# Hand-set ScalarE order in the first product of a token mixer, and sums moved to three places

## The chip, the cores and the metric

The kernel runs on one core of a Trainium2 chip. The time is device microseconds (us) of one execution; lower is better. The engines are TensorE (PE: matmuls, and PEld: its weight loads), VectorE (DVE), ScalarE (ACT), GpSimd (POOL) and SyncE (SP), which issues nearly all DMAs here. Matmuls write to PSUM, eight banks of 128 partitions x 512 fp32 values; VectorE and ScalarE read and write it too.

## The reference

The inputs are bf16: x of 2048 tokens x 1024 channels, and weights. A linear-attention block comes first, then a mixer over the tokens:

```python
x = A_x
h = x + _A_ref(_layernorm(x), A_wqkv, A_wo)        # 32 heads of 32, linear attention
h2 = h + _B_ref(_layernorm(h), B_w1, B_b1, B_w2, B_b2)

def _B_ref(x, w1, b1, w2, b2):
    h = _layernorm(x)
    u = einsum("bsd,sf->bdf", h, w1) + b1          # S=2048, F=3584, D=1024
    u = gelu(u)                                    # tanh form
    y = einsum("bdf,fs->bds", u, w2) + b2
    return y.transpose(0, 2, 1)
```

The change lies in the first of the mixer's two products, `u = gelu(h w1 + b1)`, called mixer 1 below. The second, with w2, is mixer 2.

## The kernel before

The attention block takes the first 236 us of the profiled execution, mixer 1 runs from there to about 399 us, and mixer 2 to the end.

**Seven products.** Both mixer products are cut into 2 x 2 blocks and done with seven block products in place of eight (the Winograd form of Strassen's scheme). `Product7` holds one such scheme for a pair of 128-row tiles of the output: p1 to p7, each with its left operand (weights, or sums of weights made by VectorE with `asums`) and its moving operand (the halves `hE`, `hO` of the normalized h, or their differences `hT2` to `hT4`). The accumulators are the PSUM tiles A, B and C of 512 columns. In mixer 1, p1 is in both A and B. B then takes p6 and becomes the start of C by a ScalarE copy (`copy_c`, L362). C takes p7. p5 is kept in `e`. VectorE adds `e` to C or B (`with_shared`, L425), and ScalarE's GELU (`evac`, L419) writes the finished quarter to `gE` or `gO`.

**Two at a time, and once more seven.** A `Quad` holds two such schemes, `sts[0]` and `sts[1]`. Four of its seven products, numbers 1, 5, 2 and 3, are themselves done with seven smaller products over both schemes (`Inner`, and `Inner2` for numbers 2 and 3). These are the inner products `in1`, `in5`, `in2`, `in3`. Each has steps i1 to i7 of 4 matmuls with 256 columns. The tile name in the profile is psI. The steps are chained by ScalarE: i1's result is copied to a second accumulator (L258), i6 accumulates onto it and is copied to a third (L262), and i7 accumulates onto that. i5's result is copied to SBUF (`es`, L271), or added by VectorE in `Inner2`. The ends are the `sink` functions: ScalarE copies or VectorE sums into A and B (L493, L494, L499), into `e` (L502), or into fp32 tiles `t1` (profile name t1a) and `t3` (profile name t). VectorE makes the left operands of each inner product with `sums` (profile name is, 0.4 us each). The moving operands of an inner product come from four sums of a quarter of h (`inner_moving`; for `in3` these four are `sums3`: profile names hi and hO, in the order t3, b12, t2, t4). They are made once, in the first quad of `run1`.

**The stretch.** Since steps i1 to i7 wait for each other through ScalarE, `interleave` fills the waits with the matmuls of p4, p6 and p7, which are not done in seven (512 columns each; p4 is that of the quad before). Its order is

```python
n.i1, "in", 0, n.i6, n.i2, 1, n.i5, n.i7, flush, 2, "mid", n.i3, "third", 3, n.i4, "out", flush
```

where 0 to 3 are the parts of the fill, the names are places at which the caller may put work, and `flush` does the evacuations that finished fill products have put in the list `late`. A quad u in `run1` has four such stretches: `in1` with p4 of the quad before, `in5` with three quarters of p6, `in2` with the rest of p6 and the first half of p7, `in3` with the rest of p7. Between `in2` and `in3` the code has `sts[1].with_shared(...)` and the next quad's `begin1()`, which makes two `is` sums. There are seven quads: the first in `run_first`, u = 1 to 6 in `run1`.

**Order.** The framework's scheduler orders each engine's instructions by its own estimate of readiness, except those that are passed through `pin` (`keep_in_program_order`), which are placed behind what the code has issued on that engine before. `Held` wraps an engine so that its operations are pinned while `Held.on` is set. In mixer 1 that is so for VectorE (`dve`) and TensorE (`pe`). ScalarE's are issued as `nc.scalar`, and the scheduler is free with them. Most rows of wrapped operations carry line L217 in the profile.

Of the kernel before, what the change touches and what calls it, by code (L numbers as in the profile page):

```python
# [30 lines left out]
def kernel(  # L31
# [12 lines left out]
    nc = tc.nc  # L44
# [5 lines left out]
    CW = min(BANK, D)  # L50
# [34 lines left out]
    pin = tc.keep_in_program_order  # L85
# [68 lines left out]
    def load_w2(p, pool):  # L154
        w2_tiles[p] = w_tile(pool, WLEN if pool is wpool else NF * 2 * P)[:, 0:NF * 2 * P].rearrange("p (k f) -> p k f", f=2 * P)
        nc.sync.dma_start(
            w2_tiles[p],
            B_w2[:, p * 2 * P:(p + 1) * 2 * P].rearrange("(k p) s -> p k s", p=P),
        )
# [47 lines left out]
        return {1: b11, 2: b21, 3: b22, 4: t4, 5: b12, 6: t2, 7: t3}, sums  # L207

    class Held:
        on = False  # L210

        def __init__(self, engine, always=False):
            self.engine, self.always = engine, always

        def __getattr__(self, name):
            op = getattr(self.engine, name)
            return (lambda *a, **kw: pin(op(*a, **kw))) if self.always or Held.on else op  # L217

    dve, pe = Held(nc.vector), Held(nc.tensor)
    hv, ht, hs, hd = (Held(e, True) for e in (nc.vector, nc.tensor, nc.scalar, nc.sync))  # L220

    class Inner:
# [27 lines left out]
        def i1(self):  # L250
            ae = psz.tile([P, BANK], F32, tag="z0", bufs=1, name="psI0")
            bc = psz.tile([P, BANK], F32, tag="z1", bufs=1, name="psI1")
            e, c = ae, bc
            if self.banks == 4:
                e, c = (psw.tile([P, BANK], F32, tag="w", name=f"psI{i}") for i in (2, 3))
            self.a, self.e, self.b, self.c = ae[:, 0:HW], e[:, HW:CW], bc[:, 0:HW], c[:, HW:CW]
            self.mm(1, self.a, True)
            nc.scalar.copy(self.b, self.a)  # L258

        def i6(self):  # L260
            self.mm(6, self.b, False)
            nc.scalar.copy(self.c, self.b)  # L262

        def i2(self):
            self.mm(2, self.a, False)
# [2 lines left out]
        def i5(self):  # L268
            self.mm(5, self.e, True)
            self.es = cpool.tile([P, HW], F32, tag="es", name="es")  # L270
            nc.scalar.copy(self.es[:], self.e)  # L271

        def i7(self):
            self.mm(7, self.c, False)
# [23 lines left out]
    class Product7:  # L298
# [45 lines left out]
        def p1(self):  # L344
            self.begin()
            self.mm(1, self.A, True)
            nc.scalar.copy(self.B[:], self.A[:])

        def shared_tile(self):
            self.e = cpool.tile([P, BANK], F32, tag=f"e{self.p % 2}", name="e1")  # L350
# [1 line left out]
        def p5(self, ks=None):  # L352
            if ks is None or ks[0] == 0:
                self.E = psz.tile([P, BANK], F32, tag=f"z{self.p % 2}", bufs=1, name="psE1")
            self.mm(5, self.E, True, ks)
            if self.whole(ks):
                self.shared_tile()
                nc.scalar.copy(self.e[:], self.E[:])

        def copy_c(self):  # L360
            self.C = psy.tile([P, BANK], F32, tag="y", name="psC1")
            nc.scalar.copy(self.C[:], self.B[:])  # L362

        def p6(self, ks=None, late=None):
            self.mm(6, self.B, False, ks)
# [20 lines left out]
        def p7(self, cut=None):  # L386
            self.mm(7, self.C, False)
            self.parts = [(0, CW, self.C)]
            if cut is not None:
                self.parts = [(0, cut, self.C), (cut, CW, psw.tile([P, BANK], F32, tag="w", name="psC2"))]  # L390
                nc.scalar.copy(self.parts[1][2][:, cut:CW], self.C[:, cut:CW])
            self.evac_shared(1, self.C)

        def p3(self):
# [17 lines left out]
    class Mixer1(Product7):  # L412
# [3 lines left out]

        def evac(self, fh, dh, ps, a=0, b=CW):
            ft = 2 * self.p + fh
            nc.scalar.activation(  # L419
                (gE if fh == 0 else gO)[:, self.p, dh * CW + a:dh * CW + b],  # L420
                ps[:, a:b], ACT.Gelu_apprx_tanh, bias=b1_sb[:, ft:ft + 1], scale=1.0,
            )
# [59 lines left out]
    class Quad:  # L482
# [7 lines left out]

        def sink1(self, m, h, ps):
            A, B, c = self.sts[m].A, self.sts[m].B, self.cols(h)
            nc.scalar.copy(A[:, c], ps)  # L493
            nc.scalar.copy(B[:, c], A[:, c])  # L494

        def sum1(self, m, h, ps, es):
            A, B, c = self.sts[m].A, self.sts[m].B, self.cols(h)
            dve.tensor_tensor(A[:, c], ps, es, ALU.add)
            nc.scalar.copy(B[:, c], A[:, c])  # L499

        def sink5(self, m, h, ps):
            nc.scalar.copy(self.sts[m].e[:, self.cols(h)], ps)  # L502

        def sum5(self, m, h, ps, es):
            dve.tensor_tensor(self.sts[m].e[:, self.cols(h)], ps, es, ALU.add)
# [1 line left out]
        def steps(self, *fs):  # L507
            return [(f, k) for f in fs for k in range(self.sts[0].nk)]

        def interleave(self, n, steps, at={}):  # L510
            t = len(steps)
            cuts = [0, (5 * t + 8) // 16, (9 * t + 8) // 16, (12 * t + 8) // 16, t]

            late = []

            def fill(q):
                for f, part in groupby(steps[cuts[q]:cuts[q + 1]], lambda s: s[0]):
                    f([k for _, k in part], late)

            def flush():  # L520
                while late:
                    late.pop(0)()

            for f in (
                n.i1, "in", 0, n.i6, n.i2, 1, n.i5, n.i7, flush, 2, "mid", n.i3, "third", 3, n.i4, "out", flush,
            ):
                if isinstance(f, int):
                    fill(f)
                else:
                    (at.get(f, nop) if isinstance(f, str) else f)()  # L530
# [100 lines left out]
                dve.tensor_tensor(base[:, m, c], ps, base[:, m, c], ALU.add)  # L631
            return sink

        def run1(self, pend, nxt, on_p4, before_third=nop):
            sts = self.sts
            s4, s6, s7 = self.steps(*[st.p4 for st in pend]), self.steps(*[st.p6 for st in sts]), self.steps(*[st.p7_fill for st in sts])
            c6, c7 = 3 * len(s6) // 4, len(s7) // 2

            def starting():
                self.in1.sums(slice(2, 4))  # L640
                self.asums(5)
                self.in5 = Inner(sts, 5, self.mov5, "i5", self.sink5, self.sum5)
                self.in5.sums(slice(0, 2))
                self.asums(6)
                self.t1 = self.base("t1a")
                for s, st in enumerate(sts):
                    st.begin(self.t1[:, s, :])

            self.interleave(self.in1, s4, {"in": starting, "mid": lambda: self.in5.sums(slice(2, 4))})
            self.asums(7)  # L650
            in2 = Inner2(sts, 2, self.mov2, "i1", self.add_to(self.t1), None)
            in2.sums()
            on_p4()
            nxt = nxt()
            for st in sts:
                st.shared_tile()
            self.interleave(self.in5, s6[:c6])
            sts[0].finish()
            self.asums(3)
            self.base3()  # L660
            in3 = Inner2(sts, 3, self.mov3, "i5", self.add_to(self.t3), None)
            in3.sums()
            before_third()
            sts[0].with_shared(sts[0].base3, sts[0].B)
            self.interleave(in2, s6[c6:] + s7[:c7], {
                "third": lambda: sts[0].evac(0, 0, sts[0].A), "out": lambda: sts[1].evac(0, 0, sts[1].A),
            })
            sts[1].with_shared(sts[1].base3, sts[1].B)
            if nxt is not None:
                nxt.begin1()  # L670
            self.interleave(in3, s7[c7:], {
                "third": lambda: sts[0].evac(0, 1, sts[0].base3), "out": lambda: sts[1].evac(0, 1, sts[1].base3),
            })
            return sts, nxt

    def moving(E, O, T2, T3, T4):
# [11 lines left out]
    with ExitStack() as actx:  # L688
# [21 lines left out]
        with ExitStack() as a1:  # L710
# [455 lines left out]
            for q in range(2, NVP):  # L1166
                for R in (KRun, VRun):
                    n = R(q)
# [28 lines left out]
            for b in range(NKB):  # L1197
                j0, n = b * KPB, min(KPB, ND - b * KPB)
# [28 lines left out]
        with ExitStack() as a3:  # L1227
# [143 lines left out]
            for n, (u, j) in enumerate(q_units[8:]):  # L1371
# [14 lines left out]
                if n in sums_at:  # L1386
                    cur = next(ahead)
# [58 lines left out]
    mov3, sums3 = inner_moving(hO[:, :, CW:D], NSP, inner1, "hi3")  # L1446
    NQ1 = NFP // 2

    def next_load1(u):
        def load():  # L1450
            if u < NQ1:
                load_w1(u, 0)
                load_w1(u, 1)
            else:
                load_w2(0, wpool)
        return load

    def quad1(u):
        return Quad([Mixer1(2 * u), Mixer1(2 * u + 1)], mov1, mov5, mov2, mov3)

    Held.on = True
    sums5()
    cur.mov5 = mov5
    pend, nxt = cur.run_first(quad1(1), sums1, sums2)
    for u in range(1, NQ1):
        cur = nxt
        pend, nxt = cur.run1(pend, lambda: quad1(u + 1) if u + 1 < NQ1 else None, next_load1(u + 1), sums3 if u == 1 else nop)
    Held.on = False
    for st in pend:
        st.p4()  # L1470
    mctx.close()
# [11 lines left out]
    cur = Mixer2(0)  # L1483
# [42 lines left out]
    pend = [cur, Mixer2(1)]  # L1526
    nxt = quad2(1)
# [26 lines left out]
    for u in range(1, NSP // 2):  # L1554
        cur = nxt
        last = 2 * u + 2 == NSP
        pend, nxt = cur.run2(
            pend, lambda: None if last else quad2(u + 1), after_p4(u), make_t4, CW - P if last else None,
        )
# [32 lines left out]
```

## Time and profile before

| | |
|---|---|
| median of 3 executions | 569.0 us (568.55 to 570.59) |
| the profiled execution's own time | 569.72 us |
| its span, first to last instruction | 567.9 us |
| PE / DVE / ACT busy over the span | 98% / 76% / 49% |
| granted TensorE clock | 1.00 |
| a middle quad of `run1`, from `in5`'s i6 to the next one's (312.52 to 335.38) | 22.86 us: PE 22.75, DVE 19.33, ACT 12.29 busy |
| the first quad of `run1` (264.20 to 289.66) | 25.46 us |

In a row of a timeline, the first number is the start in us from the span's start, the second the time taken; then engine, line, operation, output tile, inputs, shapes, and in brackets how long the engine stood idle before it and who released it. In a row of the waits: engine, line and tile that waited, whom for, us in total, times, longest. Matmuls are pipelined, and the last one's shown end is modelled; the distance from start to start is the surer number. In the stream a matmul of 512 columns takes 0.2165 us from start to start.

### The profile page before, as it was taken

How to read it: one execution, taken by the hardware profiler on the slowest of the kernel's cores; microseconds unless marked ns; L12 is line 12 of the kernel's file. 1: busy time of each engine (PE TensorE's matmuls, PEld its weight loads, DVE VectorE, ACT ScalarE, POOL GpSimd, SP SyncE). 2: the span in 40 equal slices, each digit the busy share in tenths (PEclk: the TensorE clock that was granted, in tenths of full speed). 3: DMA queues.
4: the chain of work that ended last, by engine and by line, in shares of the span. 5: the costliest groups of instructions: out<-in, count | busy, mean ns of one | idle time of the engine just before them, and what ended most of it. 6: DMA issues, size and time to landing. Idle time of an engine off the chain costs nothing.

```text
span 567.9 us, 8564 instructions
## 1 busy us (share of the span) xinstructions
PE 557.9 (98%) x3215; PEld 303.8 (53%) x3215; DVE 431.6 (76%) x822; ACT 280.9 (49%) x597; POOL 1.8 (0%) x8
## 2 busy tenths in 40 slices
PE   8999999999999999999899999999999999999997
PEld 3444444454444444456566766666445645645643
DVE  6898888544776788887989789788979749658725
ACT  4647777766766877635456465464220411311211
POOL 1000000000000000000000000000000000000000
PEclk9999999999999999999999999999999999999999
DMA  8833332115764852104040440422992922912111
GB/s 302 292 75 74 75 89 42 19 47 195 213 205 130 267 171 81 67 1 145 6 148 5 145 141 9 149 66 66 226 237 88 262 78 74 292 43 74 38 47 46
DMA packets 86089, 67.15 MB, mean 118 GB/s; under 512 B 15762, under 2 KB 80032, under 8 KB 86048
## 3 DMA queue, kind: packets, MB, share of 16 engines
q1 hardware_dynamic: 85312, 65.94, 40.1%
q10 hardware_dynamic: 672, 0.66, 0.3%
q8 instruction: 25, 0.41, 0.3%
q14 instruction: 16, 0.13, 0.1%
q0 software_dynamic: 64, 0.01, 0.0%
HBM read 54.54 MB, written 8.91 MB: 112 GB/s over the span
## 4 chain that ended last, share of the span: by engine, by line
PE 85%; DVE 9%; ACT 2%; DMA 2%; issue 1%; SPq 1%; DVEq 0%; ACTq 0%
PE acc_t L217 18%; PE psI L217 15%; PE psC L217 11%; PE psB L217 10%; PE psA L217 4%; PE psB L854 4%; PE psC L854 4%; PE psA L854 4%; DVE is L217 3%; PE acc_t L1129 2%; PE psB L328 2%; PE psA L328 2%; PE psE L854 2%; DVE sa L217 2%; PE psC L328 2%; DMA x_sb<-in_A_x_dram 2%
## 5 line engine op out<-in xcount | busy, mean ns | idle before, releaser
L217 PEld LDWEIGHTS <-wq 128*128 128x128 bf16 (+1 forms) x629 | 61.1, 98 | 48.3 <-issue 2.7
L217 PEld LDWEIGHTS <-sa 128*128 128x128 f16 x627 | 61.3, 98 | 35.9
L217 PEld LDWEIGHTS <-is 128*128 128x128 f16 x568 | 55.5, 98 | 27.6 <-issue 2.4
L217 PE MATMUL acc_t<-wo_sb,pqT 128*128 128x512 f16 x256 | 55.6, 379 | 0.0
L217 PE MATMUL psC<-gs,wq 128*128 128x512 f16 (+2 forms) x210 | 44.9, 365 | 0.0
L217 PE MATMUL acc_t<-xnT,wq_sb 128*128 128x512 bf16 x192 | 43.4, 379 | 0.0
L217 PEld LDWEIGHTS <-pqT 128*128 128x128 bf16 x256 | 25.0, 98 | 30.5 <-issue 0.6
L179 DVE TENSOR_SCALAR e_sb<-e_sb 128x512 bf16<-128x512 bf16 x64 | 18.6, 290 | 28.7 <-ACT e_sb L175 28.2
L175 ACT ACTIVATE e_sb<-acc_t 128x512 bf16<-128x512 f32 x40 | 23.9, 597 | 24.6 <-PE acc_t L217 12.0
L854 PEld LDWEIGHTS <-xs 128*128 128x128 f16 x208 | 20.0, 98 | 23.3 <-DVE xs L840 1.3
L217 DVE TENSOR_TENSOR ot<-ot,hr 128x512 bf16<-128x512 bf16 (+2 forms) x27 | 11.2, 414 | 28.1 <-ACT ot L469 27.7
L217 PE MATMUL psC<-hT,sa 128*128 128x512 f16 x112 | 31.2, 379 | 0.0
L217 PEld LDWEIGHTS <-wq_sb 128*128 128x128 bf16 x192 | 18.5, 98 | 23.0 <-issue 1.3
L217 PE MATMUL psI<-hi,is 128*128 128x256 f16 x200 | 30.0, 272 | 0.8 <-ACT psI L258 0.2
L258 ACT COPY psI<-psI 128x256 f32<-128x256 f32 x31 | 11.2, 362 | 38.8 <-PE psI L217 38.0
L217 PE MATMUL psB<-hT,sa 128*128 128x512 f16 x112 | 29.7, 379 | 0.0
L217 DVE BATCH_NORM_STATS2 hst<-acc_t 128x6 f32<-128x512 f32 x32 | 21.4, 692 | 9.0 <-ACT h_bf L217 8.9
L854 PE MATMUL psA<-wkv,xnT 128*128 128x512 bf16 x104 | 26.7, 379 | 0.0
L362 ACT COPY psC<-psB 128x512 f32<-128x512 f32 x22 | 12.5, 570 | 25.6 <-PE psB L217 20.9
L854 PEld LDWEIGHTS <-xnT 128*128 128x128 bf16 x156 | 15.3, 98 | 18.5 <-issue 0.2
L217 PE MATMUL psC<-hT,wq 128*128 128x512 f16 x96 | 24.6, 379 | 0.0
L217 ACT CAST h_bf<-acc_t 128x512 bf16<-128x512 f32 x32 | 18.4, 581 | 12.0 <-PE acc_t L217 12.0
(209 smaller groups left out, 1051.4 us busy)
## 6 DMA issues: line engine op xcount, KB each, us to landing
wq<-in_B_w_dram SPq DMA_DIRECT2D x14, 1024.0 KB, 7.8
wq<-in_B_w_dram SPq DMA_DIRECT2D x8, 1792.0 KB, 10.0
xr<-in_A_x_dram SPq DMA_DIRECT2D x16, 256.0 KB, 4.9
rdb<-rd_dram SPq DMA_DIRECT2D x32, 128.0 KB, 3.9
h_dram<-h_bf SPq DMA_DIRECT2D x16, 256.0 KB, 2.0
hr<-h_dram SPq DMA_DIRECT2D x32, 128.0 KB, 2.4
out_dram<-ot SPq DMA_DIRECT2D x31, 128.0 KB, 1.7
x_sb<-in_A_x_dram SPq DMA_DIRECT2D x15, 256.0 KB, 3.0
```

Source lines behind the costliest of these rows:

```text
L175: pin(nc.scalar.activation(e_sb[:], src, ACT.Exp))
L179: pin(nc.vector.tensor_scalar(e_sb[:], e_sb[:], 1.0, PHI_EPS, ALU.min, ALU.add))
L217: return (lambda *a, **kw: pin(op(*a, **kw))) if self.always or Held.on else op
L258: nc.scalar.copy(self.b, self.a)
L328: pe.matmul(ps[:, cols], lhsT=lhs[:, k, :], rhs=mv(k)[:, cols], start=(start and k == 0), stop=(k == self.nk - 1), skip_group_check=True,)
L362: nc.scalar.copy(self.C[:], self.B[:])
L854: pin(nc.tensor.matmul(ps[:], lhsT=lhs[:, k, :], rhs=rhs[:, k, :], start=(start and k == 0), stop=(k == hk2 - 1), skip_group_check=True,))
L1129: nc.tensor.matmul(qp[:, 0:SW], lhsT=wq_sb[:, kt, j * P:(j + 1) * P], rhs=xnT[:, kt, u * SW:(u + 1) * SW], start=(kt == 0), stop=(kt == ND ...
```

## The change

Four things are done:

1. A third wrapper, `act`, stands for ScalarE, with a switch of its own (`Held.scalar`), which is set for the whole of mixer 1. All ScalarE work of `Inner`, `Product7`, `Mixer1` and the sinks goes through it, so ScalarE keeps the program's order there.
2. `late` becomes one list for all stretches. A stretch of `run1` no longer flushes at its end (`keep`); the next one flushes behind its own i1, that is behind the copy L258.
3. The GELU of `sts[1]` that stood at "out" of `in2` and `in3` is put in `late` as well (`gelu_late`), behind what fill 3 has put there.
4. At u = 1, the four sums `sums3` go to three places: the first two ahead of `in5`, the third between `in2` and `in3`, the fourth at "in" of `in3`.

```diff
     class Held:
-        on = False
-        def __init__(self, engine, always=False):
-            self.engine, self.always = engine, always
+        on = scalar = False
+        def __init__(self, engine, always=False, key="on"):
+            self.engine, self.always, self.key = engine, always, key
...
-    dve, pe = Held(nc.vector), Held(nc.tensor)
+    dve, pe, act = Held(nc.vector), Held(nc.tensor), Held(nc.scalar, key="scalar")
...
             self.mm(1, self.a, True)
-            nc.scalar.copy(self.b, self.a)
+            act.copy(self.b, self.a)
...   (nc.scalar becomes act in the same way in i6, i5, p1, p5, copy_c, p7, evac, sink1, sum1, sink5)
-        def interleave(self, n, steps, at={}):
+        late = []
+
+        def interleave(self, n, steps, at={}, keep=False):
...
-            late = []
+            late = self.late
...
             for f in (
-                n.i1, "in", 0, n.i6, n.i2, 1, n.i5, n.i7, flush, 2, "mid", n.i3, "third", 3, n.i4, "out", flush,
+                n.i1, flush, "in", 0, n.i6, n.i2, 1, n.i5, n.i7, flush, 2, "mid", n.i3, "third", 3, n.i4, "out",
+                nop if keep else flush,
             ):
...
-        def run1(self, pend, nxt, on_p4, before_third=nop):
+        def run1(self, pend, nxt, on_p4, third_sums=None):
...
+            def gelu(s, dh, t):
+                return lambda: sts[s].evac(0, dh, t[:, s, :])
+
+            def gelu_late(*args):
+                return lambda: self.late.append(gelu(*args))
+
-            self.interleave(self.in1, s4, {"in": starting, "mid": lambda: self.in5.sums(slice(2, 4))})
+            self.interleave(self.in1, s4, {"in": starting, "mid": lambda: self.in5.sums(slice(2, 4))}, True)
...
-            self.interleave(self.in5, s6[:c6])
+            if third_sums is not None:
+                third_sums(slice(0, 2))
+            self.interleave(self.in5, s6[:c6], keep=True)
             sts[0].finish()
...
             in3.sums()
-            before_third()
             sts[0].with_shared(sts[0].base3, sts[0].B)
-            self.interleave(in2, s6[c6:] + s7[:c7], {
-                "third": lambda: sts[0].evac(0, 0, sts[0].A), "out": lambda: sts[1].evac(0, 0, sts[1].A),
-            })
+            self.interleave(in2, s6[c6:] + s7[:c7], {"third": gelu(0, 0, self.t1), "out": gelu_late(1, 0, self.t1)}, True)
+            if third_sums is not None:
+                third_sums(slice(2, 3))
             sts[1].with_shared(sts[1].base3, sts[1].B)
             if nxt is not None:
                 nxt.begin1()
             self.interleave(in3, s7[c7:], {
-                "third": lambda: sts[0].evac(0, 1, sts[0].base3), "out": lambda: sts[1].evac(0, 1, sts[1].base3),
-            })
+                "in": nop if third_sums is None else lambda: third_sums(slice(3, 4)),
+                "third": gelu(0, 1, self.t3), "out": gelu_late(1, 1, self.t3),
+            }, True)
...
-    Held.on = True
+    Held.on = Held.scalar = True
...
-        pend, nxt = cur.run1(..., sums3 if u == 1 else nop)
-    Held.on = False
+        pend, nxt = cur.run1(..., sums3 if u == 1 else None)
+    while Quad.late:
+        Quad.late.pop(0)()
+    Held.on = Held.scalar = False
```

More of the change, by code (lines that the diff above doesn't have):

```diff
@@ L209 @@
     class Held:
-        on = False
-        def __init__(self, engine, always=False):
-            self.engine, self.always = engine, always
+        on = scalar = False
+        def __init__(self, engine, always=False, key="on"):
+            self.engine, self.always, self.key = engine, always, key
         def __getattr__(self, name):
             op = getattr(self.engine, name)
-            return (lambda *a, **kw: pin(op(*a, **kw))) if self.always or Held.on else op
-    dve, pe = Held(nc.vector), Held(nc.tensor)
+            return (lambda *a, **kw: pin(op(*a, **kw))) if self.always or getattr(Held, self.key) else op
+    dve, pe, act = Held(nc.vector), Held(nc.tensor), Held(nc.scalar, key="scalar")
     hv, ht, hs, hd = (Held(e, True) for e in (nc.vector, nc.tensor, nc.scalar, nc.sync))
@@ L257, in i1 @@
             self.mm(1, self.a, True)
-            nc.scalar.copy(self.b, self.a)
+            act.copy(self.b, self.a)
         def i6(self):
             self.mm(6, self.b, False)
-            nc.scalar.copy(self.c, self.b)
+            act.copy(self.c, self.b)
         def i2(self):
@@ L270, in i5 @@
             self.es = cpool.tile([P, HW], F32, tag="es", name="es")
-            nc.scalar.copy(self.es[:], self.e)
+            act.copy(self.es[:], self.e)
         def i7(self):
@@ L346, in p1 @@
             self.mm(1, self.A, True)
-            nc.scalar.copy(self.B[:], self.A[:])
+            act.copy(self.B[:], self.A[:])
         def shared_tile(self):
@@ L357, in p5 @@
                 self.shared_tile()
-                nc.scalar.copy(self.e[:], self.E[:])
+                act.copy(self.e[:], self.E[:])
         def copy_c(self):
             self.C = psy.tile([P, BANK], F32, tag="y", name="psC1")
-            nc.scalar.copy(self.C[:], self.B[:])
+            act.copy(self.C[:], self.B[:])
         def p6(self, ks=None, late=None):
@@ L390, in p7 @@
                 self.parts = [(0, cut, self.C), (cut, CW, psw.tile([P, BANK], F32, tag="w", name="psC2"))]
-                nc.scalar.copy(self.parts[1][2][:, cut:CW], self.C[:, cut:CW])
+                act.copy(self.parts[1][2][:, cut:CW], self.C[:, cut:CW])
             self.evac_shared(1, self.C)
@@ L418, in evac @@
             ft = 2 * self.p + fh
-            nc.scalar.activation(
+            act.activation(
                 (gE if fh == 0 else gO)[:, self.p, dh * CW + a:dh * CW + b],
@@ L492, in sink1 @@
             A, B, c = self.sts[m].A, self.sts[m].B, self.cols(h)
-            nc.scalar.copy(A[:, c], ps)
-            nc.scalar.copy(B[:, c], A[:, c])
+            act.copy(A[:, c], ps)
+            act.copy(B[:, c], A[:, c])
         def sum1(self, m, h, ps, es):
@@ L498, in sum1 @@
             dve.tensor_tensor(A[:, c], ps, es, ALU.add)
-            nc.scalar.copy(B[:, c], A[:, c])
+            act.copy(B[:, c], A[:, c])
         def sink5(self, m, h, ps):
-            nc.scalar.copy(self.sts[m].e[:, self.cols(h)], ps)
+            act.copy(self.sts[m].e[:, self.cols(h)], ps)
         def sum5(self, m, h, ps, es):
@@ L1466 @@
         cur = nxt
-        pend, nxt = cur.run1(pend, lambda: quad1(u + 1) if u + 1 < NQ1 else None, next_load1(u + 1), sums3 if u == 1 else nop)
-    Held.on = False
+        pend, nxt = cur.run1(pend, lambda: quad1(u + 1) if u + 1 < NQ1 else None, next_load1(u + 1), sums3 if u == 1 else None)
+    while Quad.late:
+        Quad.late.pop(0)()
+    Held.on = Held.scalar = False
     for st in pend:
```

## The prediction, made before the changed kernel was run

> **What bounds the kernel now.** I read the page first, then who waited for whom on TensorE, then the timelines of one middle quad (312.52 to 335.38 us) and of the first quad of `run1` (263 to 290 us).
>
> ```profile
> PE 557.9 (98%) x3215; PEld 303.8 (53%) x3215; DVE 431.6 (76%) x822; ACT 280.9 (49%) x597; POOL 1.8 (0%) x8
> ```
>
> TensorE is busy throughout. An edit to ScalarE's order matters only where it opens or closes a TensorE gap. The waits of TensorE itself, over the span:
>
> ```profile
> PE psI L217 <- DVE t1a L217: 2.4, 1, 2.4
> ...
> PE psI L217 <- ACT psI L258: 0.2, 1, 0.2
> ```
>
> The first is one gap, in the quad u=1: `in2`'s i4 starts at 276.36 instead of 273.9, since VectorE ran the four sums of `sums3` (271.39 to 274.17) before it read i7's bank. The second is the u=1 case of a gap that comes back in every quad. The timeline of a middle quad shows it, ScalarE first:
>
> ```profile
> 310.94 0.38 ACT L499 COPY psB<-t1a 128x256 f32<-128x256 f32 x1 [0.68 <-DVE t1a L217]
> 311.25 0.68 ACT L419 ACTIVATE gO<-psC,b_sb 128x512 f16<-128x512 f32 x1
> 311.83 0.36 ACT L493 COPY t1a<-psI 128x256 f32<-128x256 f32 x1
> 312.09 0.39 ACT L258 COPY psI<-psI 128x256 f32<-128x256 f32 x1
> 312.39 0.38 ACT L494 COPY psB<-t1a 128x256 f32<-128x256 f32 x1
> ```
>
> `in5`'s first copy (L258) starts at 312.09, and i6, which accumulates onto it, at 312.52, 0.43 later. Its four fill matmuls before it started at 311.38 and take 4 x 0.2165 us, so it could have started at 312.25. The gap is 0.27 us. A quad is 22.86 us long, so apart from this gap there is nothing for ScalarE to win in it.
>
> The third view is the same quad where `in2` hands over to `in3`, the place that decides: ScalarE's rows, VectorE's, and one of TensorE.
>
> ```profile
> 323.15 0.36 ACT L258 COPY psI<-psI 128x256 f32<-128x256 f32 x1 [0.20 <-PE psI L217]
> 323.42 0.72 ACT L419 ACTIVATE gE<-t1a,b_sb 128x512 f16<-128x512 f32 x1
> 324.04 0.71 ACT L419 ACTIVATE gO<-e,b_sb 128x512 f16<-128x512 f32 x1
> 324.66 0.37 ACT L262 COPY psI<-psI 128x256 f32<-128x256 f32 x1
> ```
>
> ```profile
> 322.71 0.42 DVE L217 TENSOR_TENSOR t1a<-psI,t1a 128x256 f32<-128x256 f32 x1 [0.52 <-PE psI L217]
> 323.06 0.68 DVE L217 TENSOR_TENSOR e<-psC,e 128x512 f32<-128x512 f32 x1
> 323.65 0.68 DVE L217 TENSOR_TENSOR t<-psB,e 128x512 f32<-128x512 f32 x1
> 324.25 0.41 DVE L217 TENSOR_TENSOR is<-wq 128x512 f16<-128x512 bf16 x1
> 324.70 0.42 DVE L217 TENSOR_TENSOR is<-is,wq 128x512 f16<-128x512 f16 x1
> ```
>
> ```profile
> 325.34 0.60 PE L217 MATMUL psI<-hi,is 128*128 128x256 f16 x4
> ```
>
> The last row is `in3`'s i7. It accumulates onto what L262 copies. L262 ends at 325.03, so i7 has 0.3 us to spare. The e row ends at 323.74, in time for gO<-e.
>
> **Copies ahead of the evacuations.** The flush that used to close a stretch now stands behind the next stretch's i1. Between `in1` and `in5` ScalarE's order becomes L499, L493, L494, L258, then the GELU of psC: L494 also moves ahead of L258, as the order is now the program's. With the spacings in the rows (L499 to next 0.31; a copy to one that reads its result 0.40, as 307.08 to 307.48 earlier in the quad; L494 to next 0.32) L258 starts at 310.94 + 0.31 + 0.40 + 0.32 = 311.97 instead of 312.09. That is 0.12 us per quad, not 0.27, because L499 is released by VectorE, whose queue does not change there. Five quads (u=2 to 6): -0.6 us. Bounds: 0 and 5 x 0.27 = 1.35; I take the row sum.
>
> **Moving sums in three places (u=1 only).** The first two fall into VectorE's idle 2.14 us ahead of 266.86; they cost 1.4 us there and nothing on the path. Without the other two before `in2`'s sums, VectorE reaches them as early, measured from its last `is` sum, as in a middle quad, where i4 does not wait. That takes out the 2.45 us gap. The third and fourth (0.6 us of queue each) go to the hand-over to `in3`, counted below.
>
> **What the same edit does at the hand-over to `in3`.** Three things are put in a row there that were not before. First, `evac_shared` (VectorE's `e`, then ScalarE's GELU gO<-e) was flushed at the end of `in2`. Now it stands behind `with_shared` and `begin1`'s two sums, since these are written between the two stretches and VectorE keeps program order. VectorE's rows become: t1a 322.71, t 323.06, is 323.66, is 324.11, e 324.45. The e row ends at 324.45 + 0.68 = 325.13, 1.39 us later than now (0.60 + 0.45 + 0.34). Second, in the flush, gO<-e comes ahead of gE<-t1a, because `evac_shared` was queued in fill 3 and the GELU only at "out". Third, with ScalarE pinned, L262 (in i6, after the flush) cannot go ahead of either. So after L258 ScalarE idles until e is there: gO 325.16, gE 325.78 (0.62 per GELU, as in the rows), L262 326.40. The copy takes 0.36 and TensorE starts about 0.04 behind it: i7 at 326.80 instead of 325.34. **1.46 us per quad.** Queued behind the waiting gO are gE and L262; for L262 waits i7, and for i7 all of TensorE, which is in order. Nothing refunds it: i4, VectorE's sinks and the next `in1` follow i7 at the same distances as now, and VectorE's chain to L499 in the next quad starts from `in3`'s i4, so it moves along.
>
> That ScalarE does not pass a waiting instruction is seen in the first timeline: the psC that the GELU of 311.25 reads was complete about 310.7, ScalarE was idle from 310.3 to 310.94, and yet the GELU ran behind L499. The Trainium skill (TensorE: Matmul & The Clock Gate, under "Architectural detail: the array is 16x 32x32, not 1x 128x128", on engine queue depths) says that ScalarE's and VectorE's queues are strict first in, first out. By that rule the whole 1.46 us stands; if a ready copy could pass, this term would be nothing and the change a gain. The row bears on 0.2 us only, and agrees.
>
> By quad, as the shift of TensorE's stream:
> - u=2 to 5: 4 x 1.46 = +5.84.
> - u=6 has no next quad, so no `begin1`: only `with_shared` stands ahead of e. The e row ends at 391.64 + 0.60 + 0.68 = 392.92, gO 392.95, gE 393.57, L262 394.19, i7 at 394.59 instead of 393.92: +0.67.
> - u=1: i4 at about 273.88 (273.76 without a wait, +0.1 carried in from the next item); then t1a 274.51, the third sum 274.86, t 275.47, is 276.07, is 276.52, e 276.86 to 277.54, gO 277.57, gE 278.19, L262 278.81, i7 at 279.21. Now it is at 279.62: -0.41. Of the 2.45 us won, 2 are given back at once. The fourth sum runs 277.46 to 278.15, ahead of i4, which needs it after 280.
> - The first `in1` (u=1): the last GELU of `run_first` now precedes L258. Its e ends at 256.93, GELU 256.96, L258 257.58 instead of 256.68, i6 at 258.0 instead of 257.56: 0.43, of which the wait at 264.20 takes back all but 0.1. It is inside the -0.41.
>
> Other places where a copy moves back are covered: `in1`'s L262 from 306.59 to 306.93 (i7 needs it by 307.7), the first copy of p6 to psC from 315.33 to 317.8 (p7 begins at 319.04, 0.65 to spare), the second to about 319.1 (used after 322.9). If one cover failed it would cost 0.1 to 0.6 us a quad. After the loop the last GELU comes about 1 us later for mixer 2's differences, which TensorE first reads 5 us on. The w1 loads on SP's queue keep their place after `in1`.
>
> **Sum:** -0.41 - 0.60 + 5.84 + 0.67 = +5.5 us. The profiled execution took 569.72 us (span 567.9, 1.8 around it), which becomes 575.2; it stands 0.7 above the median of 569.0, so the forecast is 574.5 us. Bounds of this case: copies 0 to -1.35, u=1 from 0 to -2.4, and 0.2 us either way in each of four gaps: +2 to +7.
>
> **Rivals.** (1) *The copy is not caught behind the GELUs*, because e is ready in time. Then u=1 keeps about 2.3 us and the copies 0.6: -2.9, 566.1 us, faster. It decides at one row: L262 must start by 324.94, so e must end by 323.67, where it ends at 323.74 now. For it speaks that ScalarE is only half busy; against it, three VectorE instructions written ahead of e. The same time comes out if the new order does not bind ScalarE. (2) *Half of the delay*: `begin1`'s two sums do not stand ahead of e. Then each middle quad pays 0.67 as u=6 does, and u=1 0.79 less: -1.20 - 0.60 + 5 x 0.67 = +1.6, 570.6, no change that can be told. Against it: VectorE's rows are today in written order throughout. (3) *A second wait*: `in1`'s L262, also behind two GELUs now, or the psC copy loses its cover. 0.5 us in six quads, +3 more, 577.5.
>
> **How the numbers follow.** Forecast case 0.82, rival 1 0.08, rival 2 0.05, rival 3 0.05. About 0.5% (2.8 us) is what a measurement of this kernel can tell from no change. Slower by more: the forecast case but for its lowest end (0.80) and rival 3, 0.85. Same: rival 2 and that end, 0.07. Faster 0.08. The range 571 to 577 leaves out rivals 1 and 2 and the last part of 3.
>
> **What would show it.** Quads of u=2 to 5 some 24.2 us long instead of 22.86; in each a TensorE gap near 1.5 us ahead of i7 of `in3`, put down to ScalarE's L262; ScalarE idle there ahead of gO<-e, waiting for VectorE's e; no 2.4 us gap ahead of `in2`'s i4 at u=1. The gap ahead of `in5`'s i6 should be near 0.15. I am wrong if gE or L262 runs ahead of gO<-e, or e ahead of the `is` sums.

## The result and the profile after

The changed kernel takes 585.6 us (median of four runs, 585.1 to 585.7) against 568.8 us before: ratio 1.0288, 95% interval 1.0265 to 1.0310. That is 16.8 us slower. The forecast was 574.5 us, slower by 5.5, and its range ended at 577. The direction was right; the size was a third of what came. Most runs of the kernel before lie near 568.4 us at a mean granted clock of 1.000 and near 570.6 us at 0.997, so its median differs from set to set below (570.08, 570.57 and 568.43 us).

The profiled execution took 585.12 us, 15.4 more than that of before. TensorE's stream reached mixer 1 1.4 us earlier in it (234.25 instead of 235.62), so mixer 1 itself became 16.8 us longer. The page's first part:

```profile
PE 559.2 (96%) x3215; PEld 303.6 (52%) x3215; DVE 433.1 (74%) x822; ACT 282.1 (48%) x597; POOL 1.8 (0%) x8
```

The work is the same and the gaps are new. TensorE's own waits over the span:

```profile
PE psC L217 <- ACT psC L217: 11.1, 6, 1.9
PE psI L217 <- ACT psI L217: 7.3, 6, 1.7
```

The second line is the forecast gap ahead of `in3`'s i7, five times, and once 0.35 us at the first `in1`. The wait for VectorE's t1a (2.4 us, once) is gone, as forecast. The first line is in no term of the forecast sum: six times, once in each quad of `run1`, a fill matmul into psC waits for ScalarE. (The profile takes the shown end of the matmul before as the start of a wait. From start to start the gap is 2.01 us.) A middle quad, in the windows view (length, then busy time of PE, PEld, DVE, ACT and POOL with counts, granted clock, DMA share and GB/s), now lasts 26.18 us instead of 22.86:

```profile
315.95:342.13 26.18, 23.01 (x161) 15.64 (x160) 19.61 (x40) 12.52 (x29) 0.00 (x0) 1.00 0.26 82
```

In the timeline of that quad, this is the unforeseen gap: ScalarE, VectorE, TensorE.

```profile
320.93 0.36 ACT L217 COPY psI<-psI 128x256 f32<-128x256 f32 x1
323.86 0.57 ACT L217 COPY psC<-psB 128x512 f32<-128x512 f32 x1 [2.58 <-DVE t L217]
324.34 0.36 ACT L217 COPY psI<-psI 128x256 f32<-128x256 f32 x1
```

```profile
321.67 0.42 DVE L217 TENSOR_TENSOR is<-sa 128x512 f16<-128x512 f16 x1
322.13 0.43 DVE L217 TENSOR_TENSOR is<-is,sa 128x512 f16<-128x512 f16 x1
322.47 0.42 DVE L217 TENSOR_TENSOR is<-sa 128x512 f16<-128x512 f16 x1
322.81 0.42 DVE L217 TENSOR_TENSOR is<-sa,is 128x512 f16<-128x512 f16 x1
323.14 0.68 DVE L217 TENSOR_TENSOR t<-psB,e 128x512 f32<-128x512 f32 x1
```

```profile
322.03 0.60 PE L217 MATMUL psI<-hO,wq 128*128 128x256 f16 x4
324.48 0.81 PE L217 MATMUL psC<-hT,sa 128*128 128x512 f16 x3 [1.85 <-ACT psC L217]
```

ScalarE is free at 321.3. Its next instruction, `copy_c` of `sts[0]` (psC<-psB), starts at 323.86, right behind VectorE's `with_shared` (t<-psB,e), which ends at 323.82. Both only read psB. p7 accumulates onto that psC, so it starts at 324.48. It could have gone at 322.47, four half-width matmuls after 322.03.

The hand-over to `in3` in the same quad looks as the prediction drew it:

```profile
328.59 0.36 ACT L217 COPY psI<-psI 128x256 f32<-128x256 f32 x1 [0.34 <-PE psI L217]
330.60 0.72 ACT L217 ACTIVATE gO<-e,b_sb 128x512 f16<-128x512 f32 x1 [1.66 <-DVE e L217]
331.23 0.71 ACT L217 ACTIVATE gE<-t1a,b_sb 128x512 f16<-128x512 f32 x1
331.84 0.36 ACT L217 COPY psI<-psI 128x256 f32<-128x256 f32 x1
```

```profile
328.15 0.42 DVE L217 TENSOR_TENSOR t1a<-psI,t1a 128x256 f32<-128x256 f32 x1 [0.66 <-PE psI L217]
328.49 0.68 DVE L217 TENSOR_TENSOR t<-psB,e 128x512 f32<-128x512 f32 x1
329.09 0.41 DVE L217 TENSOR_TENSOR is<-wq 128x512 f16<-128x512 bf16 x1
329.54 0.42 DVE L217 TENSOR_TENSOR is<-is,wq 128x512 f16<-128x512 f16 x1
329.88 0.68 DVE L217 TENSOR_TENSOR e<-psC,e 128x512 f32<-128x512 f32 x1
```

```profile
332.26 0.60 PE L217 MATMUL psI<-hi,is 128*128 128x256 f16 x4 [1.31 <-ACT psI L217]
```

e is behind `with_shared` and two is sums, gO waits for e, gE and the copy L262 stand behind gO, and i7 waits for L262. From i5's start at 330.34 (0.435 long) the gap is 1.48 us.

And this is what the edit was to bring, at the change from `in1` to `in5`:

```profile
314.54 0.38 ACT L217 COPY psB<-t1a 128x256 f32<-128x256 f32 x1
314.85 0.37 ACT L217 COPY t1a<-psI 128x256 f32<-128x256 f32 x1
315.25 0.38 ACT L217 COPY psB<-t1a 128x256 f32<-128x256 f32 x1
315.56 0.34 ACT L217 COPY psI<-psI 128x256 f32<-128x256 f32 x1
315.82 0.69 ACT L217 ACTIVATE gO<-psC,b_sb 128x512 f16<-128x512 f32 x1
```

The copy L258 stands ahead of the GELU, behind three copies, and i6 starts at 315.95 with a gap of 0.10 us instead of 0.27.

### The profile page after: what moved, and what is told of

The parts are those of the page before. It is cut to its first block, busy times and chain, and to the rows that moved or that the text cites. A ratio compares the mean times of both kernels' runs of the same rounds, so it can differ in the third digit from the quotient of the medians.

```text
span 583.3 us, 8561 instructions
## 1 busy us (share of the span) xinstructions
PE 559.2 (96%) x3215; PEld 303.6 (52%) x3215; DVE 433.1 (74%) x822; ACT 282.1 (48%) x597; POOL 1.8 (0%) x8
## 4 chain that ended last, share of the span: by engine, by line
PE 88%; DVE 8%; ACT 2%; issue 1%; ACTq 0%
PE acc_t L217 17%; PE psI L217 16%; PE psC L217 14%; PE psB L217 9%; PE psA L217 4%; PE psB L865 4%; PE psC L865 4%; PE psA L865 4%; PE acc_t L789 2%; DVE is L217 2%; PE acc_t L1140 2%; PE psB L328 2%; PE psA L328 2%; PE psE L865 2%; PE psC L328 2%
## 5 line engine op out<-in xcount | busy, mean ns | idle before, releaser
L217 PE MATMUL psC<-hT,sa 128*128 128x512 f16 x112 | 31.2, 379 | 11.1 <-ACT psC L217 11.1
L217 DVE TENSOR_TENSOR t1a<-psI,t1a 128x256 f32<-128x256 f32 (+1 forms) x30 | 14.3, 476 | 14.7 <-PE psI L217 13.6
L217 ACT CAST h_bf<-acc_t 128x512 bf16<-128x512 f32 x32 | 18.4, 582 | 11.9 <-PE acc_t L217 11.7
L176 ACT ACTIVATE r_sb<-acc_t 128x512 bf16<-128x512 f32 x40 | 23.7, 592 | 0.0
```

Source lines behind the costliest of these rows:

```text
L176: pin(nc.scalar.activation(r_sb[:], src, ACT.Relu))
```

## The experiments

The theory after this reading has two parts. **A**: two readers of one PSUM bank on two engines keep the order in which the code writes them. In the kernel before, the flush at the end of `in5` wrote `copy_c` first; now `with_shared` is first, and it sits behind `in5`'s sums, `finish`, `asums(3)` and four is sums in VectorE's queue. **The hand-over**: the 1.48 us are what the prediction said. The rivals to A: the copy waits for its output bank psC (B), or a held ScalarE costs this by itself (C). Ratios are to the median of the kernel before in the same set; where its two clocks matter, kernels or their profiled executions are compared with each other.

**a1: the copy written first again.**

```diff
-            self.interleave(self.in5, s6[:c6], keep=True)
+            self.interleave(self.in5, s6[:c6])
```

> The changed kernel with one thing undone: in5 flushes at its own end again, so the p6 copy of sts[0] (psC<-psB) is written ahead of with_shared, which reads the same psB on VectorE. Theory A (two readers of one PSUM bank, on two engines, keep the order in which the code writes them, so the copy waits for a VectorE instruction that is 4 us late): the gap of 2.0 us ahead of p7 goes in six quads, -12 us; the copy now stands ahead of in2's L258, +0.1 us a quad: about 574 us. Rival B (the copy waits for VectorE because of its output bank psC, whose earlier tenant VectorE still reads): the wait stays, 585 us. Rival C (the gap is the price of ScalarE being held at all): 583 to 586 us.

Measured: 573.70 us, ratio 1.0071 (1.0048 to 1.0093), 11.9 us under the changed kernel. The psC line is gone from TensorE's waits and the psI line stays to the digit:

```profile
PE psI L217 <- ACT psI L217: 7.3, 6, 1.7
```

So rival C is out: ScalarE is held here as well.

**a2: `with_shared` written behind the late copy.**

```diff
-            sts[0].with_shared(sts[0].base3, sts[0].B)
             self.interleave(in2, s6[c6:] + s7[:c7], {
+                "in": lambda: sts[0].with_shared(sts[0].base3, sts[0].B),
                 "third": gelu(0, 0, self.t1), "out": gelu_late(1, 0, self.t1),
             }, True)
```

> The changed kernel with with_shared of sts[0] written at "in" of in2, that is behind the flush with the late copy. VectorE's queue keeps its order and its times; only which of the two readers of psB is written first is swapped. Theory A: the copy waits for nothing but its turn, 6 x 2.0 us go, 573.5 us. Rival B or C: no change, 585 us. If VectorE's lateness by itself were the cause, also no change.

Measured: 573.33 us, ratio 1.0063 (1.0041 to 1.0086). ScalarE's rows at this place:

```profile
316.97 0.36 ACT L217 COPY psI<-psI 128x256 f32<-128x256 f32 x1
317.24 0.58 ACT L217 COPY psC<-psB 128x512 f32<-128x512 f32 x1
```

The late copy runs right behind L258, 0.27 us after its start, as the prediction had assumed for it. VectorE's order is the same as in the changed kernel. What differs is which of the two reads is written first. Being late was therefore no fault of the copy's new place in ScalarE's order.

**a3: `with_shared` without the read of psB.**

```diff
-            sts[0].with_shared(sts[0].base3, sts[0].B)
+            sts[0].with_shared(sts[0].base3, sts[0].e)
```

> The changed kernel with with_shared of sts[0] reading e (SBUF) twice in place of psB and e: the B part of that sum is left out. It writes the same tile, at the same place in VectorE's order. Theory A (the read of the bank is what the copy waits for): the 2.0 us gap goes, 573.5 us. If the copy waited for the output tile t or for e, the gap would stay, 585 us.

Measured: 573.51 us, ratio 1.0071 (1.0049 to 1.0094). The written order is that of the changed kernel, the output tile is the same, and only the read of the bank is gone; so is the gap. The copy now runs 1.9 us ahead of `with_shared`:

```profile
317.44 0.58 ACT L217 COPY psC<-psB 128x512 f32<-128x512 f32 x1
```

```profile
319.38 0.69 DVE L217 TENSOR_TENSOR t<-e 128x512 f32<-128x512 f32 x1
```

This leaves A. In the built programs, in all six quads, the copy waits for a semaphore of VectorE in the changed kernel; in the kernel before, VectorE's instruction waits for one of ScalarE. The wait is thus drawn when the program is built. Whether the chip could do both reads at once was not tried, and as psB fills its bank, these runs do not tell whether the order is kept by bank or by tile. The Trainium skill (PSUM — Partial Sum Buffer, under "Terms", PSUM bank) says that two engines at one bank and the same 32 partitions at once are a collision, reads against reads included. No run here shows such a collision; the page gives a reason for keeping the two apart, and the runs show the price, 2.0 us a quad.

**a4: e ahead at the hand-over.**

```diff
-            sts[1].with_shared(sts[1].base3, sts[1].B)
-            if nxt is not None:
-                nxt.begin1()
+            def hand_over():
+                sts[1].with_shared(sts[1].base3, sts[1].B)
+                if nxt is not None:
+                    nxt.begin1()
+                if third_sums is not None:
+                    third_sums(slice(3, 4))
...
-                "in": nop if third_sums is None else lambda: third_sums(slice(3, 4)),
+                "in": hand_over,
```

> The changed kernel with with_shared of sts[1] and begin1 moved from between in2 and in3 to "in" of in3, so that VectorE makes e of sts[0] ahead of them. The theory of the prediction (e is late behind three VectorE instructions, gO waits for e, and L262 waits behind gO): the gap of 1.48 us ahead of in3's i7 shrinks to about 0.1 in u=2 to 5 (-5.6 us), to 0.45 at u=1 (-1.4): 578.5 us. The 2.0 us gap ahead of p7 stays. If the GELUs themselves, not the wait for e, held L262 up: a gap of 1 us stays, 584 us.

Measured: 578.83 us, ratio 1.0161 (1.0137 to 1.0184), 6.8 under the changed kernel where 7.1 were expected. ScalarE's rows:

```profile
327.02 0.36 ACT L217 COPY psI<-psI 128x256 f32<-128x256 f32 x1 [0.34 <-PE psI L217]
327.64 0.72 ACT L217 ACTIVATE gO<-e,b_sb 128x512 f16<-128x512 f32 x1 [0.26 <-DVE e L217]
328.27 0.71 ACT L217 ACTIVATE gE<-t1a,b_sb 128x512 f16<-128x512 f32 x1
328.88 0.36 ACT L217 COPY psI<-psI 128x256 f32<-128x256 f32 x1
```

The order on ScalarE is the same. The wait for e fell from 1.66 to 0.26 us, and with it the wait of i7; the psC waits stayed at 11.1 us in six.

**b4: the changed kernel with ScalarE left to the scheduler.**

```diff
-    Held.on = Held.scalar = True
+    Held.on = True
```

> The changed kernel with ScalarE left to the scheduler (Held.scalar stays off); the written order, so VectorE's order and the order of the two readers of psB, is that of the changed kernel. In the built program in3's L262 then stands ahead of gO<-e. If the 1.48 us gap comes from L262 standing behind the GELU that waits for e, it goes (1.4 us in four quads, about 1.8 at u=1), the 2.0 us gap ahead of p7 stays in six quads, and in5's i6 is 0.17 us later again in five: 585.6 - 7.4 + 0.85 = 579 us. If the hold has nothing to do with it: 585 us. If the hold were the whole loss: 567 us.

Measured: 578.89 us, ratio 1.0171 (1.0148 to 1.0195). The scheduler puts L262 ahead of gO<-e:

```profile
326.33 0.36 ACT L258 COPY psI<-psI 128x256 f32<-128x256 f32 x1 [0.34 <-PE psI L217]
326.60 0.73 ACT L419 ACTIVATE gE<-t1a,b_sb 128x512 f16<-128x512 f32 x1
327.47 0.36 ACT L262 COPY psI<-psI 128x256 f32<-128x256 f32 x1
328.34 0.72 ACT L419 ACTIVATE gO<-e,b_sb 128x512 f16<-128x512 f32 x1 [0.51 <-DVE e L217]
```

TensorE's psC waits are 11.1 us here too. So the 1.48 us needs both, the late e and the held order, and either remedy removes it; at u=1 a wait of 0.6 us for VectorE's t is left in b4. The 2.0 us does not need the hold.

**b5: the late copy alone, in the kernel before.** `interleave` takes the list and a `keep` flag as arguments; `in5` keeps its list unflushed, and `in2` flushes it behind i1. ScalarE is free.

```diff
-            self.interleave(self.in5, s6[:c6])
+            late = []
+            self.interleave(self.in5, s6[:c6], {}, late, True)
...
             self.interleave(in2, s6[c6:] + s7[:c7], {
                 "third": lambda: sts[0].evac(0, 0, sts[0].A), "out": lambda: sts[1].evac(0, 0, sts[1].A),
-            })
+            }, late)
```

> The kernel before with one part of the change alone: the p6 copy of sts[0] is written behind in2's i1 instead of at the end of in5. ScalarE is not held. Theory A (written order of the two readers of psB): the copy waits for with_shared although the scheduler is free with ScalarE, six gaps of 2.0 us ahead of p7: +12 us, 581 us. Rival C (the gap needs a held ScalarE): no change, 569 us.

Measured: 582.87 us, ratio 1.0223 (1.0203 to 1.0242), which is 12.3 us over its set's 570.57. One copy moved past another engine's read costs most of the loss. TensorE's wait:

```profile
PE psC L217 <- ACT psC L362: 13.9, 6, 4.6
```

The longest, 4.6 us, is u=1: there the copy waits for the four moving sums as well, which in this kernel still stand ahead of `with_shared`. After it TensorE ran at half its clock for some 3.4 us (four matmuls of 256 columns take 0.86 us from start to start, where 0.435 is usual):

```profile
275.00:276.00 1.00, 1.00 (x6) 0.74 (x5) 0.00 (x0) 0.00 (x0) 0.00 (x0) 0.50 0.00 0
```

Between the profiled executions, mixer 1 is 13.9 us longer than in the kernel before: 10.1 for the five gaps of 2.02, 2.2 at u=1 (4.80 in place of 2.60, from start to start), and 1.6 for the lower clock.

**b2: the moving sums alone, in the kernel before.**

```diff
+            if third_sums is not None:
+                third_sums(slice(0, 2))
             self.interleave(self.in5, s6[:c6])
...
-            before_third()
...
+            if third_sums is not None:
+                third_sums(slice(2, 3))
             sts[1].with_shared(sts[1].base3, sts[1].B)
...
             self.interleave(in3, s7[c7:], {
+                "in": nop if third_sums is None else lambda: third_sums(slice(3, 4)),
```

> The kernel before with the moving sums in three places alone (two ahead of in5, the third between in2 and in3, the fourth at "in" of in3). The gap of 2.45 us ahead of in2's i4 at u=1 goes and nothing else moves: -2.4 us, 566.5 us. Rival: VectorE is as late in in3 as it was in in2, and the gain is given back at i4 of in3: 569 us.

Measured: 566.97 us, ratio 0.9941 (0.9928 to 0.9953). This part gains, but less than the expected 2.4 us: the wait of that size is gone, and a smaller one has come, at `in3`'s i6, for the third sum.

```profile
PE psI L217 <- DVE hi L217: 0.6, 1, 0.6
```

From start to start the 2.60 us ahead of `in2`'s i4 became 0.79 ahead of `in3`'s i6 and 0.18 at a later step, 1.6 us in all, so a part of the rival came true. The ratio shows more, as most runs of the kernel before in this set were at the clock of 0.997; against its two at 1.000 (568.4) the gain is 1.4 us.

**b3: ScalarE held alone, in the kernel before.** All of ScalarE's work in mixer 1 goes through `act`; flushes and sums are as before.

```diff
-    Held.on = True
+    Held.on = Held.scalar = True
```

> The kernel before with ScalarE held in written order in mixer 1 and nothing else. The evacuations are then written ahead of the next stretch's L258 in all four stretches. From the rows of before: L258 late by 0.46 us for in5, 0.8 for in1, 1.2 for in3, 0.1 for in2, each a gap ahead of i6: 2.6 us a quad, 16 us in six, 584.5 us. If part of it overlaps, 578 us. Rival: the scheduler's order and the written one hardly differ in effect, 570 us.

Measured: 581.90 us, ratio 1.0206 (1.0189 to 1.0223); 584.5, a ratio of 1.028, was expected. In written order the GELUs of a finished stretch stand ahead of the next one's L258, and i6 waits four times a quad (from start to start 0.62, 0.08, 1.23 and 0.80 us for `in5`, `in2`, `in3` and `in1`):

```profile
PE psI L217 <- ACT psI L217: 8.9, 11, 1.1
PE psI L217 <- DVE is L217: 2.8, 6, 0.5
```

The second line is `in5`'s, and the profile names VectorE; but in a middle quad that sum ended at 316.15, and the copy L258 at 316.76, just ahead of i6 at 316.82. The four are 2.73 us a quad; less the 0.27 that was there, 2.46, near the 2.6 expected. The total falls short of six times that because the quad u=6 has only 0.19 us in `in3` and no `in1` behind it; all gaps of the profiled execution add up to 13.2 us more than before, and 568.4 + 13.2 = 581.6. The run shows what the late flush is for: with a held ScalarE it is needed. The scheduler, left free, had put L258 ahead of the GELUs in `in1` and `in3` by itself.

**b1: both waits mended.** a2 and a4 together, the late GELU put at the head of the list (so gE<-t1a, which is ready, runs ahead of gO<-e), and three moving sums ahead of `in5`:

```diff
-                return lambda: self.late.append(gelu(*args))
+                return lambda: self.late.insert(0, gelu(*args))
...
-                third_sums(slice(0, 2))
+                third_sums(slice(0, 3))
```

> The changed kernel with both waits taken out: with_shared of sts[0] at "in" of in2, with_shared of sts[1] and begin1 at "in" of in3, the late GELU of t1a/t3 put ahead of evac_shared in the list, and the first three moving sums ahead of in5. What is left of the change is the earlier copy L258 (0.17 us in five quads, -0.85), the sums at u=1 (-2.45) and 0.17 lost at the first in1: -3.1 us, 565.7 us. If a held ScalarE costs something by itself: 569 us or more.

Measured: 566.09 us, ratio 0.9927 (0.9912 to 0.9941), faster than the kernel before (568.4 us at the clock of 1.000); b2 in the same set took 566.97, 0.9 more. Not all of that is the ScalarE order, since b1 also has the third sum ahead of `in5`. Between the profiled executions b1's stream is 1.3 us shorter than b2's: 0.85 from the copies, 0.6 from the third sum, less 0.17 at the first `in1`. The new ScalarE order by itself is thus worth about 0.7 us. What TensorE still waits for in mixer 1:

```profile
PE psI L217 <- ACT psI L217: 0.4, 1, 0.4
...
PE psI L217 <- DVE t L217: 0.2, 1, 0.2
```

**c1: b1, and the last evacuation of `run_first` behind `in1`'s copy.**

```diff
-            for st in sts:
-                st.p3()
+            sts[0].p3()
+            sts[1].p3_mm()
+            self.late.append(sts[1].p3_evac)
```

> The mended kernel (b1_all_mended), and the last evacuation of run_first also behind the first in1's copy L258, where a gap of 0.51 us stood. Of it 0.2 to 0.35 us reach the end, the rest is taken up ahead of in5's i6: 565.8 us against 566.1. If VectorE's e is the later one there: no change, 566.1.

Measured: 565.45 us, ratio 0.9936 (0.9916 to 0.9957). The wait of 0.4 us in b1's list is gone. It is the fastest of the kernels run. In its profiled execution the gap of 0.51 us is gone and the others are those of b1, so all of it reaches the end, more than the 0.2 to 0.35 expected. The medians of b1 and c1, from different sets, lie 0.6 us apart.

## Why the prediction was wrong, by its own steps

**The step that failed** is the list of covers: "Other places where a copy moves back are covered: ... the first copy of p6 to psC from 315.33 to 317.8 (p7 begins at 319.04, 0.65 to spare)". The copy was costed by ScalarE's queue alone. It had been moved past another engine's reader of the same bank, and a2 and a3 show that this made it wait. In the trace of before, all three times were to be seen, the copy, `with_shared` and p7:

```profile
315.33 0.57 ACT L362 COPY psC<-psB 128x512 f32<-128x512 f32 x1 [0.28 <-PE psB L217]
```

```profile
319.72 0.68 DVE L217 TENSOR_TENSOR t<-psB,e 128x512 f32<-128x512 f32 x1
```

```profile
319.04 0.81 PE L217 MATMUL psC<-hT,sa 128*128 128x512 f16 x3
```

`with_shared` stands just behind four is sums. Placed behind it, the copy would end at about 321.0, two us after p7's 319.04. The missing term is 6 x 2.01 = 12.1 us; a1, a2, a3 take out 11.9, 12.3 and 12.1. Rival 3 had named the psC copy losing its cover, but at 0.5 us in six quads, a quarter of what it was.

The other terms, as shifts of TensorE's stream in the profiled executions, the start of mixer 1 set equal:

| term | predicted | measured |
|---|---|---|
| earlier L258, five quads | -0.60 (0.12 each) | -0.85 (0.17 each) |
| hand-over, u=2 to 5 | +5.84 (1.46 each) | +5.92 (1.48 each) |
| u=1 up to `in3`'s i7, without the psC gap | -0.41 | -0.35 |
| hand-over, u=6 | +0.67 | about 0 |
| p7 behind `with_shared`, six quads | none | +12.06 |
| sum | +5.5 | +16.8 |

The copies gained 0.05 us a quad more than forecast: L258 stands behind L499 as the row sum had it (1.02 us, 1.03 forecast), but takes 0.34 us in place of 0.39. The u=6 term vanished for TensorE: p4 of the last quad is issued behind the loop, with `Held.on` off, and three of its matmuls (psC<-hT,wq, 408.88) now stand ahead of `in3`'s i5 and fill the time until L262 is done. "Rivals" asked whether the copy L262 escapes the GELUs; it does so in b4, where ScalarE is free, and it does not in the changed kernel. The prediction's signs of being right (a gap near 1.5 us ahead of `in3`'s i7, ScalarE idle ahead of gO<-e, no wait ahead of `in2`'s i4, a gap near 0.15 ahead of `in5`'s i6) all came, except that the quads are 26.2 us long and not 24.2.

## What to carry to other kernels

When an instruction is moved in the written order, list every tile it reads and writes, and every instruction on another engine that it passes with one of these tiles in common; a read passed by a read counts too where the tile is in PSUM, as psB shows (for SBUF tiles it was not tried). Price the pair from the trace of before: where the other reader now runs is the earliest time for the one put behind it. And an engine that is held in written order makes each wait in its list a wait for all behind it, so put what is ready ahead of what waits (here gE ahead of gO, and the copy ahead of both).

## What was not expected of the hardware

Two instructions that only read the same PSUM bank, one on ScalarE and one on VectorE, did not overlap: the copy started 0.04 us behind the end of VectorE's read (323.86 and 323.82), after ScalarE had stood idle for 2.58 us. The runs show that the built program orders them; they do not show what the chip would do without.

In b5 a TensorE pause of 4.6 us was followed by some 3.4 us at a granted clock of 0.50; the pauses of 1.85 us in the changed kernel left the clock at 1.00. The kernel before has a pause of 2.45 us at u=1. Its runs at 0.997 would fit such a stretch (half the clock for 3.4 us of 568 is 0.003), and of the other kernels only b3, which has that pause too, shows a run below 0.999 (0.996). But the profiled execution of before kept 1.00 there, so for its other runs this is not shown.
